# First MoE: activation through Arctan and Sin, in groups of eight steps

## The chip, the cores and the metric

The kernel runs on one core of a Trainium2 chip. Times are microseconds of device time for one execution; "the time" is the median of three runs. TensorE multiplies, VectorE and ScalarE and GpSimd (DVE, ACT and POOL in the rows) work element by element, SyncE's queue (SP) issues all DMAs. PEld is TensorE's load of a stationary operand, which overlaps its multiplying (PE).

## The reference

Three layers over 8 batches of 576 tokens. Packed attention makes 32 packed values per head, and the tokens attend to them. Its result x, 4608 x 512, passes through two feed-forward layers:

```python
h = x @ w_in                                   # 512 -> 2048, weights in float64
sp = np.where(h > 20.0, h, np.log1p(np.exp(np.minimum(h, 20.0))))
g = h * np.tanh(sp)
x2 = g @ w_out                                 # 2048 -> 512
...
logits = x2 @ w_gate                           # second MoE: one of 8 experts per token
expert_idx = np.argmax(logits, axis=1)
for e in range(8):
    ye = np.maximum(xe @ w1[e], 0.0) @ w2[e]   # xe: the tokens of expert e
    out[expert_idx == e] = gate_w * ye
```

## The kernel before, in words

Every float32 product of the two MoEs runs as three matmuls: each operand is split into hi, rounded to 12 bits, and lo, the rest, and hi*hi, hi*lo and lo*hi are summed in PSUM. A split costs one copy (hi) and one two-input subtraction (lo).

Three stages follow each other and overlap at their ends. In the start the keys are attended (Exp on ScalarE), the float64 weights are loaded as 64-bit words and turned into float32 pairs (`convert`), and w_in is multiplied with the packed values (`fold`), so that the first MoE starts from W' = packed values x w_in, one W' per batch, which goes through DRAM (`wp_d`, `wraw`) and is split into `wp` by `get_wp`.

The first MoE works through 16 halves of a batch, 288 tokens each, and 16 steps of 128 middle columns per half: 256 steps. `attend(i)` makes the tokens' split probabilities of a half (scores on TensorE, then VectorE, GpSimd and one Exp on ScalarE). `moe1(n)` makes a pair of steps. `product` multiplies W' with the probabilities into one of two PSUM banks h (six matmuls, L626). The tanh of h/2 goes to `z` (L647) and h itself to `hs` (a copy, L233 or L234), which frees the bank. The activation h * tanh(softplus(h)) is then worked out for both steps of the pair, 128 x 576: with z = sigmoid(-h)^2 = ((1 - tanh(h/2)) / 2)^2 it is h (1 - z) / (1 + z). That takes a Square (L652), an Exp (L654) as a seed of the reciprocal and its scaling (L658), three two-input passes on VectorE (L661, L666, L669), another Square between them (L664), and the split of the result into `g` (a copy, L233, L234 or L236, and a subtraction, L245). `back` multiplies g with w_out into four accumulators (twelve matmuls a step, L637). At the end of a half they are evacuated to `x2f` (L693) and stored.

The second MoE loads one expert per batch, splits its weights (`exh`, `exl`), and does 24 matmuls for each of 128 steps (L885, L905), with a Relu (L892) and one VectorE pass (L897) between them. The gates of the experts need one Exp per half (L763).

The order of the work on every engine is written out ahead by `Plan`. Each `step` names the engines that may do it with an estimated cost, the steps it comes after, the tiles it takes from rings and gives back, and a due time. `Plan.run` plays this through: of the steps that are ready and have their buffers, each engine takes the one that is due first, and where two or three engines could do a step, the one that would end first. The costs set the order alone; on the chip each engine works down its own list and waits for semaphores. `RINGS` holds the number of tiles (h=2, z=3, hs=2, g=2, acc=4). Step n of the first MoE is due at B0 + n * TB (TB = 2897 ns), the outputs LAG = 6 steps later; the second MoE's steps come TC = 3838 ns apart. `copy_ways` lets ScalarE, VectorE or (not from PSUM) GpSimd copy, `tensor_ways` lets GpSimd or VectorE combine two tensors.

ScalarE reads its functions from a loaded table set, and a load is put into the program wherever the next function isn't in the set at hand. The program before has one, ahead of line 218: Exp, Tanh, Square, Relu and Copy all run on it.

## Time and profile before

| | us |
|---|---|
| median of three runs | 1430.24 (1426.92 to 1431.38) |
| span of the profiled execution | 1426.1 |
| TensorE busy (PE) | 1262.9 |
| VectorE busy | 949.8 |
| ScalarE busy | 718.9 |
| GpSimd busy | 575.5 |

The profile is of one execution. A busy share is an average over the three stages, so it has to be read by stretch. A row of the timeline gives the start, the duration, the engine and the line of an instruction, and in brackets how long its engine sat idle ahead of it and what released it. A row of the group table gives the line, engine, operation, tiles out<-in, shapes and count, then the busy time and the mean of one in ns, then the idle time of the engine just before them and what ended it. Matmuls overlap: one of 288 columns has a duration of about 0.3 us but starts 0.13 us after the one ahead.

### The profile page before, as it was taken

What the parts mean: (1) busy time and instruction counts of PE and PEld (TensorE: products, weight loads), DVE (VectorE), ACT (ScalarE), POOL (GpSimd) and SP (SyncE); (2) the same over time, 40 slices, a digit from 0 to 9 for tenths busy, and PEclk for the clock granted to TensorE, in tenths of its full rate; (3) what the DMA queues carried; (4) which work ended last, traced back from release to release, by engine and by line L of the source; (5) the groups of instructions that cost most, each with busy time, mean ns of one, the idle gap of its engine ahead of it and who ended that gap; (6) DMA issues with size and microseconds to landing.
All of it is one profiled execution on the core that took longest, in us unless ns stands there. A gap on an engine that the chain in (4) does not pass through costs nothing.

```text
span 1426.1 us, 23170 instructions
## 1 busy us (share of the span) xinstructions
PE 1262.9 (89%) x8680; PEld 1142.7 (80%) x8681; DVE 949.8 (67%) x1562; ACT 718.9 (50%) x1520; POOL 575.5 (40%) x506
## 2 busy tenths in 40 slices
PE   7776667779889999899998899979999999999997
PEld 4442335568888898888988889879999999999997
DVE  4845455798798786987869878884655456356341
ACT  5553334556676776767777677662323223123120
POOL 2624234574555545555455555572312122022020
PEclk9785558899999999999999999999999999999999
DMA  9854344520021201212012120121525235235130
GB/s 322 293 188 166 132 159 149 192 92 18 32 79 49 78 2 49 78 48 78 2 49 79 49 86 9 56 84 51 169 83 177 95 104 184 74 125 176 43 120 36
DMA packets 59407, 144.51 MB, mean 101 GB/s; under 512 B 6553, under 2 KB 7577, under 8 KB 59289
## 3 DMA queue, kind: packets, MB, share of 16 engines
q1 hardware_dynamic: 59288, 142.97, 29.2%
q8 instruction: 70, 1.15, 0.3%
q14 instruction: 49, 0.39, 0.1%
HBM read 107.23 MB, written 34.66 MB: 99 GB/s over the span
## 4 chain that ended last, share of the span: by engine, by line
PE 35%; DVE 28%; DMA 20%; ACT 7%; issue 5%; POOL 4%; SPq 1%; POOLq 0%; DVEq 0%; ACTq 0%
PE h_p L885 10%; PE y L905 10%; PE x2p L637 8%; DMA eraw<-w 7%; DVE z L661 5%; DVE z L669 5%; DMA word<-w_out 4%; DVE z L666 4%; PE h L626 4%; DMA wp_d<-wst 4%; DMA word<-w_in 2%; ACT z L664 2%; DVE wp L245 2%; DVE g L245 2%; DVE r L658 2%
## 5 line engine op out<-in xcount | busy, mean ns | idle before, releaser
L637 PE MATMUL x2p<-g,woh 128*128 128x288 f32 x2048 | 434.5, 303 | 23.8 <-POOL g L245 17.0
L637 PEld LDWEIGHTS x2p<-g,woh 128*128 128x128 f32 x2048 | 335.9, 192 | 41.9 <-POOL g L245 27.3
L637 PE MATMUL x2p<-g,wol 128*128 128x288 f32 x1024 | 305.7, 299 | 0.9 <-POOL wol L245 0.9
L626 PE MATMUL h<-hl,wp 128*128 128x288 f32 x1536 | 259.5, 308 | 46.3 <-DVE hs L234 19.7
L626 PEld LDWEIGHTS h<-hl,wp 128*128 128x128 f32 x1536 | 226.8, 197 | 58.5 <-ACT hs L233 23.9
L905 PE MATMUL y<-g,exh 128*128 128x288 f32 x1024 | 212.7, 299 | 3.5 <-DVE os L911 3.5
L637 PEld LDWEIGHTS x2p<-g,wol 128*128 128x128 f32 x1024 | 196.7, 192 | 1.2 <-POOL wol L245 1.2
L892 ACT ACTIVATE g<-h_p 128x288 fp32r<-128x288 f32 x128 | 51.9, 406 | 235.4 <-PE h_p L885 209.2
L905 PEld LDWEIGHTS y<-g,exh 128*128 128x128 f32 x1024 | 163.8, 188 | 7.1 <-issue 4.6
L666 DVE SCALAR_TENSOR_TENSOR z<-z,r 128x576 f32<-128x576 f32 x128 | 110.0, 859 | 82.7 <-ACT z L664 82.7
L897 DVE SCALAR_TENSOR_TENSOR g<-h_p,g 128x288 fp32r<-128x288 f32 x128 | 58.1, 454 | 151.2 <-ACT g L892 151.0
L885 PE MATMUL h_p<-x,exh 128*128 128x288 f32 x768 | 156.0, 295 | 0.0
L245 POOL TENSOR_TENSOR g<-z,g 128x576 fp32r<-128x576 f32 x80 | 145.9, 1824 | 17.0 <-ACT g L233 10.7
L905 PE MATMUL y<-g,exl 128*128 128x288 f32 x512 | 151.8, 296 | 0.0
L664 ACT ACTIVATE z<-z,b_m 128x576 f32<-128x576 f32 x128 | 99.4, 777 | 99.6 <-DVE z L661 99.3
L661 DVE SCALAR_TENSOR_TENSOR z<-z,r 128x576 f32<-128x576 f32 x128 | 134.5, 1051 | 14.4 <-POOL r L658 13.3
L647 ACT ACTIVATE z<-h 128x288 f32<-128x288 f32 x256 | 103.1, 404 | 49.2 <-PE h L626 46.8
L885 PEld LDWEIGHTS h_p<-x,exh 128*128 128x128 f32 x768 | 122.9, 188 | 0.0
L669 DVE SCALAR_TENSOR_TENSOR z<-z,hs 128x576 f32<-128x576 f32 x128 | 118.2, 923 | 3.7
L658 POOL TENSOR_SCALAR r<-r 128x576 f32<-128x576 f32 x75 | 59.8, 797 | 137.1 <-ACT r L654 124.9
L654 ACT ACTIVATE r<-z 128x576 f32<-128x576 f32 x128 | 88.0, 688 | 51.0 <-DVE z L666 50.1
L885 PE MATMUL h_p<-x,exl 128*128 128x288 f32 x384 | 112.8, 294 | 0.0
(153 smaller groups left out, 2038.0 us busy)
## 6 DMA issues: line engine op xcount, KB each, us to landing
eraw<-w SPq DMA_DIRECT2D x128, 256.0 KB
wraw<-wp_d SPq DMA_DIRECT2D x60, 256.0 KB
wp_d<-wst SPq DMA_DIRECT2D x48, 256.0 KB
k<-kT SPq DMA_DIRECT2D x16, 640.0 KB
q<-qT SPq DMA_DIRECT2D x32, 288.0 KB
x_d<-x2f SPq DMA_DIRECT2D x16, 576.0 KB
x2f<-x_d SPq DMA_DIRECT2D x16, 576.0 KB
out<-os SPq DMA_DIRECT2D x16, 576.0 KB
```

What stands on the lines that cost most here:

```text
L245: engine.tensor_tensor(out=d, in0=a(), in1=b(), op=op)
L626: T.matmul(out=h, lhsT=wp_t[b, c][:, xw, kt, 128 * (o + k):128 * (o + k) + 128], rhs=a2[i][:, xa, kt], start=(m == 0), stop=(m == 5))
L637: T.matmul(out=accs[i, d], lhsT=w_o[c][xw][:, o + k, 128 * d:128 * d + 128], rhs=t["g"][:, xg, k], start=(f + k == 0 and m == 0), stop=(f ...
L647: z1.append(step("ACT", 291, lambda k=k: S.activation(out=part("z", k), in_=t["p", k], func=AF.Tanh, scale=0.5), after=[ins[n + k], *z1], ...
L654: r0 = step("ACT", 573, lambda: S.activation(out=new("r0"), in_=t["z"], func=AF.Exp, scale=SEED_A), after=[z2], takes=key("r0"), due=due)
L658: engine.tensor_scalar(out=t["r0"], in0=t["r0"], scalar1=SEED_B, scalar2=SEED_C, op0=ALU.mult, op1=ALU.add)
L661: e1 = step("DVE", 669, lambda: V.scalar_tensor_tensor(out=t["z"], in0=t["z"], scalar=1.0, in1=t["r0"], op0=ALU.add, op1=ALU.mult), after= ...
L664: e2 = step("ACT", 573, lambda: S.activation(out=t["z"], in_=t["z"], func=AF.Square, bias=b_m15), after=[e1], due=due)
L666: e3 = step("DVE", 669, lambda: V.scalar_tensor_tensor(out=t["z"], in0=t["z"], scalar=0.75, in1=t["r0"], op0=ALU.add, op1=ALU.mult), after ...
L669: g0 = step("DVE", 669, lambda: V.scalar_tensor_tensor(out=t["z"], in0=t["z"], scalar=-0.5, in1=t["hs"], op0=ALU.add, op1=ALU.mult), after ...
L885: T.matmul(out=h_p, lhsT=ex_t[ek, c][xw][:, k, 128 * o:128 * o + 128], rhs=x2s[xk][:, xx, k], start=(n == 0), stop=(n == 11))
L905: T.matmul(out=accs[xk, d], lhsT=ex_t[ek, 2 + c][xw][:, o, 128 * d:128 * d + 128], rhs=hc[xk, f][:, xh], start=(f == 0 and n == 0), stop=( ...
```

## The change

The activation becomes h * sin(pi/2 - 2 arctan((1 - tanh(h/2)) / 2)), since sin(pi/2 - 2 arctan y) = (1 - y^2) / (1 + y^2). For a pair it is, after the same tanh and copy, an Arctan and a Sin on ScalarE, in place in `z`, and one multiplication on VectorE with `hs`. The two Squares, the Exp, its scaling and two of the three VectorE passes go; `r0` and its ring go with them. The factor 2 of the evacuations is no longer needed.

`moe1` now makes a group of eight steps. First come all eight products with their tanh and copies; the tanh also come after every Sin of the group before (`sins`). Then a Sin of one column (`tables`) stands for the load of the table set, after all the group's tanh; then each pair's Arctan and Sin. The Exp of `attend` and of the first two gates are put between groups by `sins` and `trig_after`. The rings become z=5, hs=4, g=4, the lag of the outputs is a group, and `attend(i + 1)` is planned after the first group of half i.

In the first MoE `tensor_ways(..., False)` leaves two-input passes to VectorE alone: the three of `attend`, the subtraction of `g`, and that of `wp` for all batches but the first. The planner's cost of a matmul goes from 122 to 133 ns (798 for a product, 399 and 1596 for others), TB to 2394, TC to 3192; products within a group are due TI = 798 ns apart. The scratch of dynamic DMAs shrinks. The diff, cut to its core:

```diff
-SEED_A, SEED_B, SEED_C = -1.39926343, 0.65662738, 0.33973963
+GROUP = 8
+HALF_PI = 1.5707963267948966
...
-             q=2, s2=1, mx2=1, sm2=1, at2=1, hl=2, z=3, hs=2, r0=1, g=2, g2=4, x2f=1,
+             q=2, s2=1, mx2=1, sm2=1, at2=1, hl=2, z=5, hs=4, g=4, g2=4, x2f=1,
...
-    def tensor_ways(dst, a, b, op, n):
+    def tensor_ways(dst, a, b, op, n, pool=True):
...
-        return [("Pool", 148 + 2.104 * n, on(G)), ("DVE", 69 + 1.042 * n, on(V))]
+        return [("Pool", 148 + 2.104 * n, on(G))] * pool + [("DVE", 69 + 1.042 * n, on(V))]
...
-    LAG = 6
+    LAG = GROUP
...
-                                               lambda kt=kt: r32(wp_t[b, c][:, 0, kt]), ALU.subtract, 512),
+                                               lambda kt=kt: r32(wp_t[b, c][:, 0, kt]), ALU.subtract, 512, b == 0),
...
+        ex = step("ACT", 573, lambda: S.activation(out=t["s2"], in_=t["s2"], func=AF.Exp, scale=scale),
+                  after=[m3] + sins.get(2 * i - 2, []), due=due)
+        trig_after[2 * i - 1].append(ex)
...
-        z2 = step("ACT", 573, lambda: S.activation(out=t["z"], in_=t["z"], func=AF.Square, bias=b_half, scale=-0.5),
-                  after=z1, due=due)
-        r0 = step("ACT", 573, lambda: S.activation(out=new("r0"), in_=t["z"], func=AF.Exp, scale=SEED_A),
-                  after=[z2], takes=key("r0"), due=due)
-
-        def seed(engine):
-            engine.tensor_scalar(out=t["r0"], in0=t["r0"], scalar1=SEED_B, scalar2=SEED_C, op0=ALU.mult, op1=ALU.add)
-
-        r1 = plan.step([("Pool", 641, lambda: seed(G)), ("DVE", 369, lambda: seed(V))], after=[r0], due=due)
-        e1 = step("DVE", 669, lambda: V.scalar_tensor_tensor(out=t["z"], in0=t["z"], scalar=1.0, in1=t["r0"],
-                                                             op0=ALU.add, op1=ALU.mult),
-                  after=[r1, z2], due=due)
-        e2 = step("ACT", 573, lambda: S.activation(out=t["z"], in_=t["z"], func=AF.Square, bias=b_m15),
-                  after=[e1], due=due)
-        e3 = step("DVE", 669, lambda: V.scalar_tensor_tensor(out=t["z"], in0=t["z"], scalar=0.75, in1=t["r0"],
-                                                             op0=ALU.add, op1=ALU.mult),
-                  after=[e2], frees=key("r0"), due=due)
-        g0 = step("DVE", 669, lambda: V.scalar_tensor_tensor(out=t["z"], in0=t["z"], scalar=-0.5, in1=t["hs"],
-                                                             op0=ALU.add, op1=ALU.mult),
-                  after=[e3, *hc], frees=key("hs"), due=due)
-        g1 = plan.step(copy_ways(lambda: new("g", (128, 2, 2, TK), F32R)[:, 0], lambda: t["z"], 2 * TK), after=[g0],
-                       takes=key("g"), due=due)
-        last_g1 = g1
-        g2 = plan.step(tensor_ways(lambda: t["g"][:, 1], lambda: t["z"], lambda: r32(t["g"][:, 0]), ALU.subtract, 2 * TK),
-                       after=[g1], frees=key("z"), due=due)
...
+        for n in pairs:
+            c = n % 16 // 4
+            z1[n], hc[n] = [], []
+            for k in range(2):
+                at_k = due + (n + k - n0) * TI
+                ins[n + k] = step("PE", 798, lambda n=n, k=k: product(n, k),
+                                  after=wp_done[b, c] + a2_done[i] + [after_in(n + k - 1)],
+                                  takes=[("h", n + k)], frees=[("wa", ("w", b, c))] * (hf == 1 and (n + k) % 4 == 3)
+                                  + [("hl", i)] * ((n + k) % 16 == 15), due=at_k)
+                z1[n].append(step("ACT", 291, lambda n=n, k=k: tanh(n, k), after=[ins[n + k], *z1[n]] + sins.get(gr - 1, []),
+                                  takes=[("z", n)] * (k == 0), due=at_k))
+                hc[n].append(plan.step(copy_ways(lambda n=n, k=k: part(n, "hs", k), lambda n=n, k=k: tiles[n]["p", k], TK, True),
+                                       after=[z1[n][k], *hc[n]], takes=[("hs", n)] * (k == 0), frees=[("h", n + k)], due=at_k))
+                b_steps.extend([z1[n][k], hc[n][k]])
+        due += GROUP * TI
+        tables = step("ACT", 1500, lambda: S.activation(out=trig, in_=b_half, func=AF.Sin),
+                      after=[z for n in pairs for z in z1[n]] + trig_after[gr] + sins.get(gr - 1, []), due=due)
+        sins[gr] = []
+        for j, n in enumerate(pairs):
+            at_n = due + 2 * j * TI
+            z = lambda n=n: tiles[n]["z"]
+            th = step("ACT", 573, lambda z=z: S.activation(out=z(), in_=z(), func=AF.Arctan, bias=b_half, scale=-0.5),
+                      after=[tables, *z1[n]], due=at_n)
+            si = step("ACT", 573, lambda z=z: S.activation(out=z(), in_=z(), func=AF.Sin, bias=b_pi, scale=-2.0),
+                      after=[th], due=at_n)
+            sins[gr].append(si)
+            g0 = step("DVE", 669, lambda n=n, z=z: V.tensor_tensor(out=z(), in0=z(), in1=tiles[n]["hs"], op=ALU.mult),
+                      after=[si, *hc[n]], frees=[("hs", n)], due=at_n)
+            g1 = plan.step(copy_ways(lambda n=n: new(n, "g", (128, 2, 2, TK), F32R)[:, 0], z, 2 * TK), after=[g0],
+                           takes=[("g", n)], due=at_n)
+            last_g1 = g1
+            g2 = plan.step(tensor_ways(lambda n=n: tiles[n]["g"][:, 1], z, lambda n=n: r32(tiles[n]["g"][:, 0]),
+                                       ALU.subtract, 2 * TK, False),
+                           after=[g1], frees=[("z", n)], due=at_n)
+            b_steps.extend([tables, th, si, g0, g1, g2])
+            for k in range(2):
+                c, o = divmod((n + k) % 16, 4)
+                for d in range(4):
+                    outs[n + k, d] = step("PE", 399, lambda n=n, k=k, d=d: back(n, k, d),
+                                          after=[g2, outs.get((n + k - 1, d))] + split["o", c, o],
+                                          takes=[("acc", (i, d))] * (f0 == 0 and n + k == n0),
+                                          frees=[("g", n)] + [("wb", ("o", c, x)) for x in "hl"] * (i == NH - 1 and o == 3),
+                                          due=due + GROUP * TB + (2 * j + k) * (TB - TI))
+                    b_steps.append(outs[n + k, d])
+        due += GROUP * TB
...
-                S.activation(out=x2f[i][:, d], in_=accs[i, d], func=AF.Copy, scale=2.0)
+                S.activation(out=x2f[i][:, d], in_=accs[i, d], func=AF.Copy)
             else:
-                V.tensor_scalar(out=x2f[i][:, d], in0=accs[i, d], scalar1=2.0, scalar2=None, op0=ALU.mult)
+                V.tensor_copy(out=x2f[i][:, d], in_=accs[i, d])
...
-        ex = step("ACT", 113, lambda: gate_exp(i), after=[mx], due=due)
+        ex = step("ACT", 113, lambda: gate_exp(i), after=[mx, *exp_after], due=due)
+        if exp_before is not None:
+            exp_before.append(ex)
...
-    TB, TC = 2897, 3838
+    TB, TI, TC = 2394, 798, 3192
...
+    attend(0, open_b, at(-14))
-        attend(i, after_in(n0 - 17) or open_b, at(n0 - 14))
-        for c in range(4):
-            if hf == 0 and (b, c) not in wp_done:
-                get_wp(b, c, after_in(n0 + 4 * c - 28) or open_b, at(n0 + 4 * c - 12))
-            for f in range(4 * c, 4 * c + 4, 2):
-                moe1(n0 + f, at(n0 + f))
-        if i == 1:
+        for g in range(2):
+            for c in range(2 * g, 2 * g + 2):
+                if hf == 0 and (b, c) not in wp_done:
+                    get_wp(b, c, after_in(n0 + 4 * c - 28) or open_b, at(n0 + 4 * c - 12))
+            moe1(n0 + GROUP * g, at(n0 + GROUP * g))
+            if g == 0 and i + 1 < NH:
+                attend(i + 1, after_in(n0 - 1) or open_b, at(n0 + 2))
+        if i == 2:
             for m in range(2):
-                sp = split_x2(m, m, "x2b", x2_done[m], at(16 * m + 20))
-                b_steps.extend(sp + gate(m, [("x2b", m)], at(16 * m + 24)))
-
-    # the first half again, for the second MoE
+                sp = split_x2(m, m, "x2b", x2_done[m], at(16 * m + 26))
+                b_steps.extend(sp + gate(m, [("x2b", m)], at(16 * m + 28), sins[5], trig_after[6]))
...
-    nc = bacc.Bacc("TRN2", target_bir_lowering=False, num_devices=1)
+    nc = bacc.Bacc("TRN2", target_bir_lowering=False, num_devices=1, dynamic_dma_scratch_size=1024)
```

## Rows read from the trace of the kernel before

**Rows 1.** The page: the busy line, and the chain by engine.
```profile
PE 1262.9 (89%) x8680; PEld 1142.7 (80%) x8681; DVE 949.8 (67%) x1562; ACT 718.9 (50%) x1520; POOL 575.5 (40%) x506
PE 35%; DVE 28%; DMA 20%; ACT 7%; issue 5%; POOL 4%; SPq 1%; POOLq 0%; DVEq 0%; ACTq 0%
```

**Rows 2.** By tile x2p: count, duration min/median/max in ns, first and last start.
```profile
L693 ACT ACTIVATE x2f<-x2p x64: 391/424/456, 297.8 to 981.3; 128x288 f32<-128x288 f32 x64
```

**Rows 3.** By stretch: length, busy us (count) of PE, PEld, DVE, ACT, POOL, PEclk, DMA, GB/s.
```profile
298.00:981.00 683.00, 620.56 (x4439) 592.47 (x4438) 556.08 (x706) 471.17 (x952) 371.46 (x295) 0.98 0.15 52
400.00:935.00 535.00, 491.83 (x3558) 471.03 (x3556) 434.71 (x541) 379.50 (x768) 289.31 (x230) 0.99 0.16 54
```

**Rows 4.** Timeline of TensorE: two products in a row, and the scores of a half.
```profile
942.00 0.95 PE L626 MATMUL h<-hl,wp 128*128 128x288 f32 x6
944.37 0.95 PE L626 MATMUL h<-hl,wp 128*128 128x288 f32 x6
...
614.25 1.19 PE L554 MATMUL o<-q,pkb 128*64 128x288 f32 x8
615.37 0.53 PE L637 MATMUL x2p<-g,woh 128*128 128x288 f32 x2
```

**Rows 5.** Groups by line from 400 to 950 us.
```profile
L637 PEld LDWEIGHTS x2p<-g,woh 128*128 128x128 f32 x1586 | 256.6, 189 | 27.9 <-POOL g L245 23.1 <-issue 2.6 <-ACT x2f L693 1.4
L626 PEld LDWEIGHTS h<-hl,wp 128*128 128x128 f32 x1188 | 168.2, 189 | 33.2 <-DVE hs L234 18.1 <-ACT hs L233 14.9
L245 POOL TENSOR_TENSOR g<-z,g 128x576 fp32r<-128x576 f32 x65 | 119.9, 1845 | 13.6 <-ACT g L233 10.1
L661 DVE SCALAR_TENSOR_TENSOR z<-z,r 128x576 f32<-128x576 f32 x99 | 104.6, 1057 | 12.3 <-POOL r L658 11.4
L669 DVE SCALAR_TENSOR_TENSOR z<-z,hs 128x576 f32<-128x576 f32 x99 | 92.7, 936 | 3.2
L666 DVE SCALAR_TENSOR_TENSOR z<-z,r 128x576 f32<-128x576 f32 x99 | 83.4, 843 | 72.0 <-ACT z L664 72.0
```

**Rows 6.** Timeline of VectorE: two-input passes, GpSimd quiet and at work.
```profile
617.50 0.76 DVE L245 TENSOR_TENSOR g<-z,g 128x576 fp32r<-128x576 f32 x1 [0.17 <-POOL g L236]
618.17 0.75 DVE L661 SCALAR_TENSOR_TENSOR z<-z,r 128x576 f32<-128x576 f32 x1
...
629.18 1.73 DVE L245 TENSOR_TENSOR g<-z,g 128x576 fp32r<-128x576 f32 x1
```

**Rows 7.** Timeline of ScalarE: the one table load, and passes back to back.
```profile
0.78 1.28 ACT L218 ACT_TABLE_LOAD   x1 [0.64 <-PEq L1136]
...
603.56 0.39 ACT L647 ACTIVATE z<-h 128x288 f32<-128x288 f32 x1
603.85 0.40 ACT L233 ACTIVATE hs<-h 128x288 f32<-128x288 f32 x1
...
610.45 0.76 ACT L652 ACTIVATE z<-z,b_half 128x576 f32<-128x576 f32 x1
611.12 0.39 ACT L647 ACTIVATE z<-h 128x288 f32<-128x288 f32 x1
```

**Rows 8.** Timeline: a product with its tanh and copy, and a product that waited.
```profile
640.55 0.96 PE L626 MATMUL h<-hl,wp 128*128 128x288 f32 x6
641.54 0.41 ACT L647 ACTIVATE z<-h 128x288 f32<-128x288 f32 x1 [0.42 <-PE h L626]
641.85 0.41 ACT L233 ACTIVATE hs<-h 128x288 f32<-128x288 f32 x1
...
950.36 1.07 PE L626 MATMUL h<-hl,wp 128*128 128x288 f32 x6 [0.86 <-DVE hs L234]
```

**Rows 9.** By stretch: the end of the first MoE, and the second.
```profile
950.00:968.00 18.00, 12.57 (x70) 11.88 (x71) 17.91 (x19) 8.82 (x19) 13.46 (x11) 0.81 0.20 62
1000.00:1426.00 426.00, 413.25 (x3083) 403.00 (x3081) 210.30 (x508) 106.54 (x233) 81.09 (x70) 0.99 0.34 115
```

**Rows 10.** By stretch, and a piece of the chain: the start.
```profile
283.00:298.00 15.00, 11.96 (x80) 10.28 (x80) 15.00 (x19) 8.79 (x18) 10.20 (x10) 1.00 0.21 74
...
266.54 12.51 DMA word<-w_out
```

More of the change, by code (lines that the diff above doesn't have):

```diff
@@ L633, in back, with part @@
-        def back(k, d):
-            if f + k == 0:
+        def part(n, name, k):
+            return (tiles[n][name] if k else new(n, name))[:, k]
+        def back(n, k, d):
+            f = n % 16 + k
+            c, o = divmod(f, 4)
+            if f == 0:
                 accs[i, d] = tile_of("acc", [128, TK], name=f"x2p{d}")
             for m, (xw, xg) in enumerate(((0, 0), (0, 1), (1, 0))):
-                T.matmul(out=accs[i, d], lhsT=w_o[c][xw][:, o + k, 128 * d:128 * d + 128], rhs=t["g"][:, xg, k],
-                         start=(f + k == 0 and m == 0), stop=(f + k == 15 and m == 2))
@@ L641, in moe1 @@
-        z1, hc = [], []
-        for k in range(2):
-            ins[n + k] = step("PE", 735, lambda k=k: product(k),
-                              after=wp_done[b, c] + a2_done[i] + [after_in(n + k - 1)],
-                              takes=[("h", n + k)], frees=[("wa", ("w", b, c))] * (hf == 1 and o + k == 3)
-                              + [("hl", i)] * (f + k == 15), due=due + k * TB)
-            z1.append(step("ACT", 291, lambda k=k: S.activation(out=part("z", k), in_=t["p", k], func=AF.Tanh, scale=0.5),
-                           after=[ins[n + k], *z1], takes=key("z") * (k == 0), due=due + k * TB))
-            hc.append(plan.step(copy_ways(lambda k=k: part("hs", k), lambda k=k: t["p", k], TK, True), after=[z1[k], *hc],
-                                takes=key("hs") * (k == 0), frees=[("h", n + k)], due=due + k * TB))
@@ L685, in moe1, with tanh @@
-        b_steps.extend([*hc, *z1, z2, r0, r1, e1, e2, e3, g0, g1, g2, *(outs[n + k, d] for k in range(2) for d in range(4))])
-        if f < 14:
+                T.matmul(out=accs[i, d], lhsT=w_o[c][xw][:, o, 128 * d:128 * d + 128], rhs=tiles[n]["g"][:, xg, k],
+                         start=(f == 0 and m == 0), stop=(f == 15 and m == 2))
+        def tanh(n, k):
+            S.activation(out=part(n, "z", k), in_=tiles[n]["p", k], func=AF.Tanh, scale=0.5)
+        for n in pairs:
[12 more added lines that the diff above has]
+                b_steps.extend([z1[n][k], hc[n][k]])
```

61 lines of the change are left out of this document (27 added, 34 removed).

## Prediction

> **What bounds the kernel now.** I read the page's busy line and its chain first [rows 1]. TensorE has 89% of the span, but that is an average over a start that waits for DMAs, a first MoE and a second MoE. The chain gives TensorE 35%, VectorE 28% and DMA 20%, so over long stretches it is VectorE's work that TensorE waits for. The question is how far the first MoE is from TensorE's own pace.
>
> The evacuations of its accumulators (L693) date its halves: the first half ends at 297.8 us, the last of the 16 at 981.3 [rows 2]. That is 683 us for 15 halves, 45.5 us each. The stretch table has the same stretch [rows 3]: 4439 matmuls, VectorE busy 556 of 683 us. Its row from 400 to 935 us has 3558 matmuls in 535 us; a half has 288 of the MoE and 8 for the scores, so these are 12.0 halves of 44.6 us.
>
> What would a half cost on TensorE alone? In an undisturbed stretch one product of six matmuls starts at 942.00 and the next one, behind twelve output matmuls, at 944.37 [rows 4]: 2.37 us for 18 matmuls, 0.132 us each. The scores of a half take from 614.25 to 615.37, 1.12 us. A half is 16 x 2.37 + 1.12 = 39.0 us, and a steady half loses 5.6 us. The group table of 400 to 950 us says where [rows 5]: TensorE's weight loads sit idle 27.9 us ahead of output matmuls, 23.1 of it until GpSimd's subtraction of g (L245, 1.85 us each), and 33.2 us ahead of products, nearly all until a copy of h has freed a bank. Together 61 us in 550, 11%. Both come from the activation: three two-input passes of 0.84 to 1.06 us on VectorE, with waits for other engines between them, then GpSimd's subtraction.
>
> **The change, part by part.**
>
> *VectorE.* L661 and L666 go, one multiplication stays in place of L669, and the second subtraction of g always comes to VectorE. Such a pass takes 0.67 us from its start to its successor's where GpSimd is quiet (617.50 to 618.17) and 1.73 at the worst, with GpSimd at work (629.18) [rows 6]; the mean of the slowest line is 1.06 [rows 5]. I take 0.67, because nearly all two-input work of GpSimd goes, and keep 1.06 as the other end. For 12 halves: VectorE's 434.7 us [rows 3], less 104.6 and 83.4, plus the 65 subtractions moved from GpSimd [rows 5] at 0.67 to 1.06 (44 to 69). The attention's three two-input passes and the weights' four a half are 84 in 12 halves; between none and all of them are new on VectorE (0 to 89). That is 291 to 405 us, 24 to 34 a half. Even the upper end is below 39.0: VectorE leaves the bound. GpSimd keeps only copies of g and casts.
>
> *ScalarE.* Three passes of a pair go, two come. Back to back a 576-column pass with a bias tile takes 0.67 us (610.45 to 611.12), a 288-column one from PSUM 0.29 (603.56 to 603.85) [rows 7]. Removed are two Squares at 0.67 and an Exp without bias tile, between 0.29 and 0.67: 1.63 to 2.01 us. Arctan and Sin add 1.34. ScalarE gets lighter by 0.3 to 0.7 us a pair, 2.3 to 5.4 a half. Against it stand table loads: the trace's only one takes 1.28 us [rows 7], and each group of eight steps needs two, four a half, 5.1 us. With 379.5/12 = 31.6 us a half now [rows 3] that makes 31 to 34, some 80 to 88% of TensorE's 39.0.
>
> [...]
>
> *The cycle of a group.* Grouping adds two waits: no Arctan before the last tanh of its group, no tanh before the last Sin of the group ahead. Queued behind the waiting pass on ScalarE are copies of h, and a copy that waits keeps a PSUM bank and so the next product. Phase A is eight products through two banks. A bank's round is 0.99 us from product start to tanh (640.55 to 641.54), 0.31 on to the copy, 0.41 of copy [rows 8], and at once the next product (950.36 in [rows 8] was released by such a copy): 1.7 us, some 2.0 if the copy is VectorE's and starts after the tanh's 0.41. Two banks make 0.86 to 1.0 us a product, 7 to 8 us a group. Phase B is two loads, eight passes and, as an allowance, 2 us of other copies: 2.6 + 5.4 + 2 = 10 us. The cycle is 17 to 18 us, and TensorE needs 39.0/2 = 19.5. During B it has the previous group's outputs, 8 x 1.58 = 12.7 us, which don't wait for this group's Sins. So the two waits are covered, with about 2 us to spare; each us past that would cost 1 us in each of 30 groups.
>
> *TensorE's order.* Products come in runs of eight, at 0.79 us each quicker than the banks empty (0.86 to 1.0). Outputs of the group ahead can fill the gap; unfilled it costs 0.2 x 8 = 1.7 us a group, filled nothing. The nearest row for a dense stretch is the second MoE: 413.25 busy us in 426 [rows 9], 13 lost over 16 halves. I take 1 us a half, and 0 to 2 for the range.
>
> *The start.* Up to 283 us the float64 weights set the pace (a word DMA of 12.51 us still starts at 266.54), and the change doesn't touch them. From 283 to 298 VectorE is busy all 15 us [rows 10]; less work there could give up to 8 us, and the later first outputs (a group of eight in place of a lag of six steps) could take as much. I take zero.
>
> *The end.* [...] The last group's first output is ready some 6 us after its last tanh (a load, two pairs of passes, three VectorE passes), under 12.7 us of the group ahead. [...] The second MoE runs at TensorE's pace already. The planner's new constants reorder its queues only: plus or minus 5. The smaller edits (factor 2 folded into the Sin form, a constant tile, the scratch size) are priced at nothing; VectorE's and ScalarE's spare 5 us a half cover them, and uncovered they are one small pass in the whole run.
>
> **Sum.** TensorE's own work from 298 to 981 is 4439 x 0.132 = 586 us [rows 3, 4], so 683 - 586 = 97 us can be had. Less 15 halves x 1 us: 82. The profiled span is 1426.1 us and the median of the runs 1430.24, so 4.1 us lie around the span: 1426.1 - 82 + 4.1 = **1348 us**. About 0.3%, 4 us, is what a measurement here can tell from no change.
>
> **Rivals.**
>
> *ScalarE's cycle becomes the bound.* If a switch costs more than its row, or copies of h queue behind Sins, phase B grows. At 21 us a group, 3.5 more than my cycle, a half is 42, the stretch 15 x 42 = 630 and the gain 53: 1377 us. For it: ScalarE's 80 to 88% in two phases that can't overlap. Against it: 2 us to spare and outputs to run meanwhile. [...] 20%.
>
> *Slower: tables switch inside the group.* If Arctan and Sin share no table set, or the copies between them aren't in it, nearly each of the eight passes brings a load. Nine loads in place of two make 17.5 + 7 x 1.28 = 26.5 us a group, 53 a half, 15 x 7.5 = 112 us more: 1542 us. It decides from four extra loads on, 17.5 + 4 x 1.28 = 22.6 us, the present half of 45.5. Against it: in the kernel before Exp, Tanh, Square and Copy live on one load, so functions do share sets; for the new pair no row says it. 5%.
>
> *VectorE stays the bound.* If the moved passes all run at the worst row, 1.73 us, they add 149 x 1.73 = 258 us to 434.7 - 188, 42 us a half, and with the waits between passes the halves stay near 45: 1430 us. Against it: GpSimd, which slows them, has lost its own. 3%, and 2% for gains between this and the first rival.
>
> *Full density* is the forecast's lower tail: 1426 - 97 - 8 + 4 = 1325 us.
>
> **How the numbers follow.** The forecast has 70%, with 1333 to 1364 as its own range (0 to 2 us a half, start and end as above in part). Leaving out the slow cases and the ends of the others, 1333 to 1388 holds 8 in 10: the forecast's range and the greater part of the first rival's. Faster by over 0.3%: 0.70 + 0.20 + 0.02 = 0.92; within 0.3%: 0.03; slower: 0.05.
>
> **What would show it.** Evacuations of the halves 39 to 41 us apart; 365 or more matmuls in each 50 us between 400 and 850; VectorE busy 24 to 34 us a half; 64 table loads of 1.28 us beside the first one; output matmuls that no longer wait for GpSimd. I am wrong if TensorE idles ahead of products until a tanh or a copy of h that waited for a Sin, if the loads number hundreds, or if VectorE's passes stay near 1 us.

## The result, and the profile after

The changed kernel takes 1368.84 us (median; 1366.46 to 1369.12) beside 1428.58 for the kernel before on the same chip (four runs; the 1430.24 further up is the median of three of them), a ratio of 0.9579 (95% interval 0.9555 to 0.9602). The forecast was 1348, its range 1333 to 1388: the sign and the range hold, and the time is 21 us above the forecast. Where these 21 us are is the main question of what follows.

The page first, its busy line and its chain by engine, as in [rows 1]:

```profile
PE 1252.8 (92%) x8680; PEld 1139.5 (83%) x8681; DVE 711.2 (52%) x1328; ACT 705.9 (52%) x1469; POOL 343.3 (25%) x375
PE 64%; DMA 18%; ACT 7%; DVE 6%; issue 2%; SPq 2%; POOL 1%; ACTq 0%; DVEq 0%; POOLq 0%
```

VectorE falls from 67 to 52% of the span and from 28 to 6% of the chain, and TensorE now makes 64% of the chain. The evacuations (L705 now) and two stretches answer to [rows 2] and [rows 3]; columns as there:

```profile
L705 ACT ACTIVATE x2f<-x2p x64: 410/412/414, 310.4 to 908.6; 128x288 f32<-128x288 f32 x64
...
400.00:935.00 535.00, 531.92 (x3953) 516.75 (x3952) 277.46 (x396) 385.11 (x762) 124.26 (x144) 1.00 0.18 60
...
310.40:908.60 598.20, 594.27 (x4412) 575.71 (x4411) 330.12 (x485) 445.51 (x885) 146.00 (x169) 1.00 0.18 59
```

The two evacuations date three parts. The first half ends at 310.4 us in place of 297.8 (12.6 us later). The 15 halves behind it take 598.2 us in place of 683.5 (85.3 less, 39.9 us a half). From the last evacuation to the end it is 1367.4 - 908.6 = 458.8 us in place of 444.8 (14.0 more). Of the 85.3 and of the 14.0, 3.2 us are two products of the second MoE that stood at 968 and 973 us, inside the first MoE, and now come behind it. The sum, 12.6 - 85.3 + 14.0 = -58.7, is the difference of the spans, 1426.1 to 1367.4.

The group table from 400 to 850 us answers to [rows 5]:

```profile
L646 PEld LDWEIGHTS x2p<-g,woh 128*128 128x128 f32 x1434 | 229.1, 188 | 0.0
L633 PEld LDWEIGHTS h<-hl,wp 128*128 128x128 f32 x1080 | 147.2, 188 | 13.3 <-ACT z L650 9.6 <-ACT hs L235 3.7
...
L247 DVE TENSOR_TENSOR g<-z,g 128x576 fp32r<-128x576 f32 x88 | 76.3, 881 | 30.8 <-POOL g L238 30.8
...
L678 DVE TENSOR_TENSOR z<-z,hs 128x576 f32<-128x576 f32 x89 | 64.4, 753 | 97.5 <-ACT z L675 97.5
...
L667 ACT ACT_TABLE_LOAD x23 | 29.5, 1283 | 0.4
```

Output matmuls no longer wait for anybody (27.9 us before); products wait 13.3 us in 450 for the tanh (L650) and the copy of h, 33.2 in 550 before. ScalarE's timeline over one group shows the loads:

```profile
604.39 0.41 ACT L235 ACTIVATE hs<-h 128x288 f32<-128x288 f32 x1
604.82 1.28 ACT L667 ACT_TABLE_LOAD   x1
606.11 0.20 ACT L667 ACTIVATE trig<-b_half 128x1 f32<-128x1 f32 x1
606.22 1.43 ACT L673 ACTIVATE z<-z,b_half 128x576 f32<-128x576 f32 x2
...
610.23 1.43 ACT L675 ACTIVATE z<-z,b_pi 128x576 f32<-128x576 f32 x2
611.67 1.28 ACT L650 ACT_TABLE_LOAD   x1
616.41 0.41 ACT L650 ACTIVATE z<-h 128x288 f32<-128x288 f32 x1 [3.46 <-PE h L633]
```

The load starts 0.02 us after the copy ends at 604.80, and the next pass starts at the load's end. The load back at 611.67 runs while the tanh behind it still waits for its product, so that one is hidden. There are 65 loads in all, each of 1283 ns.

### The profile page after: what moved, and what is told of

Read it like the earlier page. It is cut to its first block, busy times and chain, and to the rows that moved or that the text cites. A ratio compares the mean times of both kernels' runs of the same rounds, so it can differ in the third digit from the quotient of the medians.

```text
span 1367.4 us, 22646 instructions
## 1 busy us (share of the span) xinstructions
PE 1252.8 (92%) x8680; PEld 1139.5 (83%) x8681; DVE 711.2 (52%) x1328; ACT 705.9 (52%) x1469; POOL 343.3 (25%) x375
## 4 chain that ended last, share of the span: by engine, by line
PE 64%; DMA 18%; ACT 7%; DVE 6%; issue 2%; SPq 2%; POOL 1%; ACTq 0%; DVEq 0%; POOLq 0%
PE x2p L646 23%; PE h L633 13%; PE y L919 12%; PE h_p L899 12%; DMA wp_d<-wst 6%; DMA eraw<-w 3%; DMA word<-w_in 3%; DMA word<-w_out 2%; DMA x2f<-x_d 1%; PE o L558 1%; ACT z L673 1%; ACT z L675 1%; SPq L256 1%; DMA wraw<-wp_d 1%; PE l_p L748 1%
## 5 line engine op out<-in xcount | busy, mean ns | idle before, releaser
L646 PE MATMUL x2p<-g,woh 128*128 128x288 f32 x2048 | 420.1, 300 | 3.0 <-POOL g L238 2.0
L633 PE MATMUL h<-hl,wp 128*128 128x288 f32 x1536 | 235.5, 304 | 11.7 <-ACT hs L235 7.5
L633 PEld LDWEIGHTS h<-hl,wp 128*128 128x128 f32 x1536 | 216.2, 194 | 27.5 <-ACT z L650 11.4
L238 POOL TENSOR_SCALAR g<-z 128x576 fp32r<-128x576 f32 x118 | 100.7, 861 | 345.0 <-DVE z L678 229.4
L650 ACT ACTIVATE z<-h 128x288 f32<-128x288 f32 x256 | 105.0, 410 | 121.8 <-PE h L633 114.0
L678 DVE TENSOR_TENSOR z<-z,hs 128x576 f32<-128x576 f32 x128 | 96.3, 781 | 123.9 <-ACT z L675 123.7
L247 DVE TENSOR_TENSOR g<-z,g 128x576 fp32r<-128x576 f32 x128 | 113.6, 901 | 41.1 <-POOL g L238 41.0
L247 DVE TENSOR_TENSOR exl<-eraw,exh 128x512 fp32r<-128x512 f32 x89 | 82.2, 953 | 42.2 <-ACT exh L235 37.3
L235 ACT ACTIVATE hs<-h 128x288 f32<-128x288 f32 x248 | 100.8, 406 | 0.4 <-DVE z L678 0.4
L919 PEld LDWEIGHTS y<-g,exl 128*128 128x128 f32 x512 | 97.2, 190 | 0.0
L235 ACT ACTIVATE exh<-eraw 128x512 fp32r<-128x512 f32 x93 | 58.3, 631 | 70.6 <-DMA eraw<-w 67.4
```

Of the source, the lines that this page charges most:

```text
L235: ways = [("ACT", (51 if psum else 93) + 0.833 * n, on(lambda d, x: S.activation(out=d, in_=x, func=AF.Copy))), ("DVE", 69 + (1.03 if psum ...
L238: ways.append(("Pool", 160 + 0.835 * n, on(lambda d, x: G.tensor_scalar(out=d, in0=x, scalar1=1.0, scalar2=1.0, op0=ALU.mult, op1=ALU.mult))))
L247: engine.tensor_tensor(out=d, in0=a(), in1=b(), op=op)
L633: T.matmul(out=h, lhsT=wp_t[b, c][:, xw, kt, 128 * o:128 * o + 128], rhs=a2[i][:, xa, kt], start=(m == 0), stop=(m == 5))
L646: T.matmul(out=accs[i, d], lhsT=w_o[c][xw][:, o, 128 * d:128 * d + 128], rhs=tiles[n]["g"][:, xg, k], start=(f == 0 and m == 0), stop=(f = ...
L650: S.activation(out=part(n, "z", k), in_=tiles[n]["p", k], func=AF.Tanh, scale=0.5)
```

## The experiments

All kernels side by side. The first evacuation and the last are those of their profiles; the column behind them is the 15 halves between, then the rest of the span behind the last. The times are medians of four runs, of two for two_more_loads and groups_of_four. The ratio is to the kernel before on the same chip.

| kernel | us | ratio (95%) | first | 15 halves | rest |
|---|---|---|---|---|---|
| before | 1428.58 | | 297.8 | 683.5 | 444.8 |
| changed | 1368.84 | 0.9579 (0.9555 to 0.9602) | 310.4 | 598.2 | 458.8 |
| tc_back | 1366.25 | 0.9563 (0.9506 to 0.9619) | 310.1 | 598.2 | 456.3 |
| tc_costs_back | 1359.96 | 0.9546 (0.9482 to 0.9610) | 307.7 | 598.2 | 447.3 |
| costs_back | 1357.19 | 0.9506 (0.9472 to 0.9540) | 307.7 | 598.3 | 446.8 |
| first_half_by_four | 1377.62 | 0.9650 (0.9592 to 0.9708) | 306.4 | 607.6 | 459.7 |
| both_back | 1362.00 | 0.9536 (0.9480 to 0.9591) | 306.2 | 607.2 | 446.8 |
| first_half_as_before | 1348.15 | 0.9442 (0.9414 to 0.9471) | 298.0 | 601.2 | 443.9 |
| gpsimd_again | 1374.89 | 0.9630 (0.9588 to 0.9673) | 309.8 | 604.0 | 459.9 |
| before_vectore_alone | 1392.08 | 0.9754 (0.9712 to 0.9797) | 299.3 | 645.6 | 442.4 |
| before_two_passes_out | 1353.01 | 0.9474 (0.9433 to 0.9514) | 300.9 | 605.6 | 449.6 |
| vectore_alone_gpsimd_loaded | 1460.08 | 1.0226 (1.0175 to 1.0277) | 307.2 | 706.2 | 447.1 |
| two_more_loads | 1407.91 | 0.9860 (0.9804 to 0.9917) | 311.5 | 638.7 | 457.5 |
| groups_of_four | 1393.93 | 0.9757 (0.9718 to 0.9795) | 310.1 | 623.1 | 460.6 |

### The second MoE: the planner's constants

**tc_back** takes back only the distance of the second MoE's steps.

```diff
-    TB, TI, TC = 2394, 798, 3192
+    TB, TI, TC = 2394, 798, 3838
```

> The changed kernel with one constant of the planner set back: TC = 3838 ns, the due spacing of the second MoE's steps. The estimated costs of its matmuls stay new. Theory P: the second MoE lost 14 us (from the last evacuation to the end 458.8 us against 444.8 before) because the planner's new constants order loads and splits of the next batch later; TC alone is enough, then this stretch comes back to 445 to 450 us and the time to about 1357. Rival Q: it is not TC but the matmul costs; then the stretch stays at 456 to 461 and the time at 1369. Rival R: the loss comes from what the first MoE leaves behind (queues, buffers); then it stays as well.

The rest is 456.3 us: the distance alone brings 2.5 us and is not it.

**tc_costs_back** takes back the costs of its matmuls too, and **costs_back** these alone.

```diff
-        y_in[n] = step("PE", 1596, lambda: moe2_in(b, i, f), after=ex_done[b, c] + x2_split_done[i] + [None if early else ins[N1 - 1]],
+        y_in[n] = step("PE", 1473, lambda: moe2_in(b, i, f), after=ex_done[b, c] + x2_split_done[i] + [None if early else ins[N1 - 1]],
...
-            y_out[n, d] = step("PE", 399, lambda d=d: moe2_out(b, i, f, d),
+            y_out[n, d] = step("PE", 366, lambda d=d: moe2_out(b, i, f, d),
```

> The changed kernel with TC = 3838 ns and the second MoE's estimated matmul costs set back too (1473 and 366 ns); the first MoE is planned as in the changed kernel. Theory P and Q: the second MoE's stretch comes back to 444 to 448 us, time about 1356. Rival R (the first MoE's leavings): it stays at 456 to 461 and the time at 1369.

> The changed kernel with the planner's costs of the second MoE's matmuls alone taken back (1473 and 366 for 1596 and 399); its steps stay due 3192 ns apart. Theory C (the costs alone make the worse order in the second MoE): from the last evacuation to the end 444 to 450 us in place of 458.8, the time 1357 to 1364. Rival B (it takes both, costs and distance, to come back to the old order): 453 to 460 us, the time 1364 to 1371.

The rest falls to 447.3 and 446.8 us, so the costs alone do it, some 12 of the 14.0 us, and what the first MoE leaves behind (rival R) is not it. They emit the same matmuls in another order. The stretch from 1000 to 1300 us, the y matmuls and the VectorE share of the split of x2, first for the changed kernel, then for costs_back:

```profile
1000.00:1300.00 300.00, 290.83 (x2121) 282.69 (x2121) 151.62 (x356) 76.16 (x166) 69.35 (x55) 0.98 0.36 119
...
L919 PE MATMUL y<-g,exh 128*128 128x288 f32 x666 | 141.0, 303 | 8.1 <-DVE os L925 8.0
...
L730 DVE TENSOR_TENSOR x<-x2f,x 128x576 fp32r<-128x576 f32 x7 | 13.0, 1860 | 0.2
```

```profile
1000.00:1300.00 300.00, 295.90 (x2205) 288.35 (x2205) 156.16 (x372) 82.66 (x178) 64.19 (x57) 1.00 0.40 129
...
L919 PE MATMUL y<-g,exh 128*128 128x288 f32 x696 | 145.1, 300 | 1.8 <-DVE os L925 1.8
...
L730 DVE TENSOR_TENSOR x<-x2f,x 128x576 fp32r<-128x576 f32 x2 | 3.7, 1866 | 0.1
```

With the change's costs 84 matmuls fewer are done in 300 us. TensorE waits 8.0 us for VectorE's evacuation of y (L925), seven of the 1.86 us subtractions of L730 into x stand on VectorE where costs_back has two, and the granted clock is 0.98. Which entry of the lists starts the loss, this subtraction or the loads of the expert's weights ahead of it, no run separates. The new cost of 133 ns a matmul is what [rows 4] show, 0.132 us, and the old 122 is not: the truer cost gave the worse order.

### The start: groups against late weights

The first half's products wait for the quarters of W', which arrive one by one. The changed kernel's stretch that answers to [rows 10], then ScalarE and TensorE near 280 us:

```profile
283.00:298.00 15.00, 8.84 (x39) 7.15 (x40) 12.93 (x17) 9.16 (x17) 7.86 (x8) 0.66 0.42 138
...
250.61 0.41 ACT L650 ACTIVATE z<-h 128x288 f32<-128x288 f32 x1
...
273.77 0.63 ACT L235 ACTIVATE wp<-wraw 128x512 fp32r<-128x512 f32 x1 [5.13 <-DMA wraw<-wp_d]
274.31 0.39 ACT L650 ACTIVATE z<-h 128x288 f32<-128x288 f32 x1
...
280.11 1.28 ACT L667 ACT_TABLE_LOAD   x1
...
286.14 2.19 PE L558 MATMUL o<-q,pkb 128*64 128x288 f32 x8 [4.89 <-DMA q<-qT]
290.29 0.61 PE L646 MATMUL x2p<-g,woh 128*128 128x288 f32 x1 [1.96 <-POOL g L238]
```

The tanh at 250.61 is that of step 11, so steps 8 to 11 were ready for their Arctan at 251 us. But it comes after the tanh of steps 12 to 15. The first of these stands on ScalarE behind a cast of W' that waits 5.13 us for its DMA, and starts at 274.31; the load for the whole group is at 280.11, 29 us late for half of it. Until 290.29 TensorE has no output to make: 39 matmuls in these 15 us where before had 80, and the granted clock is 0.66 in this stretch, 1.00 before [rows 10].

**first_half_by_four** makes four groups of four of the first half, and plans the attention of the second half behind step 12 in place of step 8.

```diff
+        size = 4 if i == 0 else 8
+        for f in range(0, 16, size):
...
-            moe1(n0 + GROUP * g, at(n0 + GROUP * g))
+            moe1(n0 + f, at(n0 + f), size)
```

> The changed kernel with the first half of the first batch in four groups of four steps, all other halves in groups of eight. Theory G: the first half ends 12.6 us later than before (310.4 against 297.8 us) because the Arctans of steps 8 to 11, whose products are through at 251 us, wait for the products of steps 12 to 15, whose weights land at 273; by four, steps 8 to 11 go ahead: the half ends at 298 to 304 and the time is 1358 to 1364. Rival S: the start is set by the float64 weights' DMAs and the other order of the queues, not by the group; then the half ends at 309 to 312 and the time is 1369 or, for four more table loads of 1.28 us, up to 1374.

The first half does end 4.0 us earlier, short of the 298 to 304 expected, and the kernel is slower. From the timelines of TensorE and ScalarE:

```profile
276.32 0.43 PE L649 MATMUL x2p<-g,woh 128*128 128x288 f32 x2
...
282.34 0.68 ACT L409 ACTIVATE a<-word 128x512 f32<-128x512 f32 x1 [3.32 <-DMA word<-w_out]
282.93 0.39 ACT L653 ACTIVATE z<-h 128x288 f32<-128x288 f32 x1
...
292.69 3.25 PE L636 MATMUL h<-hl,wp 128*128 128x288 f32 x12 [5.01 <-ACT hs L235]
295.74 0.68 PE L649 MATMUL x2p<-g,woh 128*128 128x288 f32 x2
...
317.43 4.69 PE L636 MATMUL h<-hl,wp 128*128 128x288 f32 x18 [2.46 <-ACT hs L235]
```

The outputs of steps 8 to 11 do come earlier, from 276.32 in place of 290.29. But the last two tanh of the group of steps 12 to 15 stand on ScalarE behind a conversion of w_out that waits 3.32 us for its DMA (282.34). Behind them come the load, the Arctans and Sins and the split of g, two products of the second half go ahead on TensorE (292.69), and the outputs of that group start at 295.74 only. So the theory's wait is there, but taking it away brings little by itself. The second half's products wait for copies of h behind the added loads and Sins, and the second half takes 50.5 us from one first evacuation to the next (306.44 to 356.98) where the changed kernel takes 41.3 (310.41 to 351.69): nearly all of the 9.4 us by which the 15 halves are longer (607.6). **both_back** joins this with tc_costs_back:

> The first half by four and the second MoE's TC and costs set back, together. If theories G and P (or Q) both hold, the gains add up, since they lie in different stretches: 1369 - 8 - 13 = 1348 us, which is the time that was forecast for the change with neither loss. If only one holds, about 1357; if neither, 1369.

It has both effects side by side, 607.2 and 446.8 us, and misses the 1348 expected. With these constants the groups of four bring the first half's end forward by 1.5 us only (307.7 to 306.2).

**first_half_as_before** removes the group from the first half altogether: pairs, the seed by Exp, the Squares and the three VectorE passes, outputs six steps behind; groups from the second half on, and the planner's costs and distance as in tc_costs_back. The first half's own matmuls are planned at the old costs too.

```diff
-            moe1(n0 + GROUP * g, at(n0 + GROUP * g))
+                if i == 0:
+                    for f in range(4 * c, 4 * c + 4, 2):
+                        moe1_pair(f, at(f))
+            if i > 0:
+                moe1(n0 + GROUP * g, at(n0 + GROUP * g))
```

> The changed kernel with the planner's constants of the second MoE taken back (as in tc_costs_back), and with the first half alone worked as before: pairs of steps, outputs six steps behind, seed by Exp, Squares and three VectorE passes (the seed in a tile of hs), its evacuations doubled; GpSimd takes no two-input pass there either. Groups of eight from the second half on. Theory G (the start loses because a group holds the outputs of steps 8 to 15 back until W' of its last quarter is there): the first half ends at 298 to 302 in place of 307.7, the other 15 halves and the second MoE stay (598 and 447 us): span 1343 to 1347, time 1346 to 1354. Rival P (the loss of the start is the planner's order or VectorE alone, not the group): the first half still ends at 306 to 309, time 1356 to 1364. Rival L (the loss only moves: the first group of the second half then waits instead): first half at 298 to 302, but the last evacuation still at 904 to 909, time 1355 to 1364.

```profile
L793 ACT ACTIVATE x2f<-x2p x60: 410/411/415, 342.2 to 899.2; 128x288 f32<-128x288 f32 x60
L795 DVE TENSOR_SCALAR x2f<-x2p x4: 448/458/458, 298.0 to 300.5; 128x288 f32<-128x288 f32 x4
...
283.00:298.00 15.00, 15.00 (x95) 13.79 (x95) 13.24 (x18) 9.52 (x21) 8.26 (x8) 0.85 0.24 85
```

The first half ends at 298.0, TensorE is busy through the stretch (95 matmuls), and the last evacuation comes 6.7 us ahead of that of tc_costs_back: 1348.15 us. So of the 12.6 us that the start lost the group costs 9.7 (307.7 to 298.0, with the same constants of the second MoE), and the order made by those constants the rest (310.4 to 307.7). Of the 9.7 us 3.0 are lost again in the 15 halves behind (601.2 for 598.2), and the rest of the span is 3.4 us shorter (443.9 for 447.3), for which no run gives a reason. What in the group costs the 9.7 is shown in part only: ending the wait of steps 8 to 11 for the tanh of steps 12 to 15 gives 1.5 to 4.0 back in the groups of four, less what their added loads cost, and how much falls to the loads, to the Sins and to the order of the queues stays open. This kernel is faster than both the kernel before and the changed one.

### The first MoE: which part brings the 85 us

**before_two_passes_out** leaves out L661 and L666 of the kernel before, **before_vectore_alone** moves the two-input passes there to VectorE, and **gpsimd_again** lets GpSimd have them in the changed kernel.

```diff
-        e1 = step("DVE", 669, lambda: V.scalar_tensor_tensor(out=t["z"], in0=t["z"], scalar=1.0, in1=t["r0"],
...
-        e3 = step("DVE", 669, lambda: V.scalar_tensor_tensor(out=t["z"], in0=t["z"], scalar=0.75, in1=t["r0"],
...
```

> The kernel before without the two VectorE passes at L661 and L666: the pair goes from the scaled seed to the second Square and on to the last multiplication, so the activation's values are not the reference's. No groups, no table loads, GpSimd as before, planner's constants as before. Theory A (VectorE's passes and the waits between them are most of the 5.6 us that a half loses; the start and the second MoE lose nothing without groups and new constants): VectorE falls by 188 us in 12 halves, halves of 41 to 42.5 us, first half's end within 3 us of 297.8, second MoE within 4 us of 444.8: time 1365 to 1385. Rival B (GpSimd's subtraction is the stall): its 23 us in 12 halves stay, halves of 43 to 44.5: 1395 to 1415.

The group table from 400 to 850 us:

```profile
L637 PEld LDWEIGHTS x2p<-g,woh 128*128 128x128 f32 x1434 | 229.0, 188 | 8.1 <-issue 7.4 <-ACT x2f L687 0.5
...
L626 PEld LDWEIGHTS h<-hl,wp 128*128 128x128 f32 x1074 | 152.0, 188 | 5.0 <-DVE hs L234 5.0
...
L245 DVE TENSOR_TENSOR g<-z,g 128x576 fp32r<-128x576 f32 x79 | 61.7, 782 | 122.7 <-POOL g L236 122.7
...
L245 POOL TENSOR_TENSOR g<-z,g 128x576 fp32r<-128x576 f32 x11 | 15.7, 1430 | 0.9
```

Two passes less, with no table load and no group, make halves of 40.4 us, a little under theory A's 41 to 42.5, and the start and the rest stay near those of before. But the run does not set the passes apart from GpSimd: with VectorE freed, the planner gives it 79 subtractions of g in these 450 us and GpSimd 11, where GpSimd had 65 in 550 [rows 5]. Rival B's stall went with the passes.

```diff
-        return [("Pool", 148 + 2.104 * n, on(G)), ("DVE", 69 + 1.042 * n, on(V))]
+        return [("Pool", 148 + 2.104 * n, on(G))] * pool + [("DVE", 69 + 1.042 * n, on(V))]
...
-        g2 = plan.step(tensor_ways(lambda: t["g"][:, 1], lambda: t["z"], lambda: r32(t["g"][:, 0]), ALU.subtract, 2 * TK),
+        g2 = plan.step(tensor_ways(lambda: t["g"][:, 1], lambda: t["z"], lambda: r32(t["g"][:, 0]), ALU.subtract, 2 * TK, False),
```

> The kernel before with one part of the change alone: the two-input passes of the attention, of g and of W' (all batches but the first) on VectorE alone. Theory A (VectorE is the bound before, its load must fall first): VectorE gets 44 to 69 us of subtractions in 12 halves and up to 89 us of the attention's and weights' passes on top of 434.7, some 40 to 49 us a half against the present 44.6; no gain, and slower if its load passes the half: 1425 to 1490. Rival B (the wait for GpSimd's subtraction is the stall, and passes without GpSimd run at 0.67 us): the 23 us of waits in 12 halves go, 1395 to 1410.

The same stretch, 400 to 850 us:

```profile
L637 PEld LDWEIGHTS x2p<-g,woh 128*128 128x128 f32 x1382 | 222.3, 188 | 14.3 <-DVE g L245 8.4 <-issue 4.4 <-DVE z L661 0.4
...
L661 DVE SCALAR_TENSOR_TENSOR z<-z,r 128x576 f32<-128x576 f32 x87 | 73.8, 848 | 3.5 <-POOL r L658 3.1
L245 DVE TENSOR_TENSOR g<-z,g 128x576 fp32r<-128x576 f32 x87 | 71.6, 823 | 1.9 <-POOL g L236 1.3
```

This one surprised: VectorE gets more work and the halves fall to 43.0 us, 37.9 us in the first MoE; theory A fell, and 1392.08 is even a little under rival B's 1395. L661 takes 848 ns in place of 1057 [rows 5], and the wait for GpSimd's subtraction of g is gone.

For gpsimd_again the same is turned round in the changed kernel, here for g:

```diff
-                                       ALU.subtract, 2 * TK, False),
+                                       ALU.subtract, 2 * TK),
```

> The changed kernel, but GpSimd may take two-input passes in the first MoE again; groups of eight and the Arctan and Sin stay. Theory A (the gain comes from the shorter activation; the outputs of the group ahead give each subtraction of g some 12 us of cover, so a slow GpSimd subtraction costs little): the 15 halves from the first evacuation to the last stay at 598 to 613 us, the time is 1366 to 1384. Rival B (the gain comes from GpSimd no longer standing ahead of the output matmuls and slowing VectorE): the waits of the outputs for GpSimd come back, about 23 us in 12 halves, and VectorE's passes go back to about 1 us: 25 to 45 us more, 1392 to 1412.

The same stretch again:

```profile
L646 PEld LDWEIGHTS x2p<-g,woh 128*128 128x128 f32 x1414 | 225.9, 188 | 0.0
...
L247 POOL TENSOR_TENSOR g<-z,g 128x576 fp32r<-128x576 f32 x23 | 35.2, 1530 | 1.4
```

With the short activation the same freedom costs 5.8 us in 15 halves, as theory A had it. GpSimd has 23 subtractions of g in 450 us, and the output matmuls wait for none of them. So the parts overlap: moving the passes alone brings 37.9 us, the short activation in groups with GpSimd left free 79.5 (683.5 to 604.0), both together 85.3, the two products that moved being in the last two figures. But the planner used the freedom less than before: 23 subtractions in 450 us where GpSimd had 65 in 550. No run has the short activation with GpSimd's old load.

**vectore_alone_gpsimd_loaded** asks which of GpSimd's two effects before_vectore_alone removed.

```diff
+        if n // 2 % 3 < 2:
+            step("Pool", 1360, lambda: G.tensor_tensor(out=idle, in0=idle, in1=idle, op=ALU.subtract), after=[g0], due=due)
```

> As before_vectore_alone (1392.1 us; the two-input passes on VectorE alone), but GpSimd gets, in two pairs of steps of three, a subtraction of 128 x 576 of its own on a tile that nobody else reads: as much two-input work as the subtraction of g gave it before, with no TensorE work behind it. GpSimd's copies can queue behind it, and the planner sees its cost. Theory D (VectorE's passes last longer while GpSimd runs a two-input pass, and that is what the kernel before lost by them): VectorE's three passes of a pair go back from 0.77 to 0.85 us to 0.85 to 1.05, and the time to 1412 to 1440. Rival C (the loss was GpSimd's 1.85 us in the chain ahead of the output matmuls, which this kernel doesn't have): passes stay at 0.77 to 0.87 us, time 1388 to 1402.

A subtraction for which nobody waits costs 68 us, more than theory D's range (1412 to 1440), and rival C is out. From the group table from 400 to 850 us, and a piece of the timeline of VectorE and GpSimd:

```profile
L663 DVE SCALAR_TENSOR_TENSOR z<-z,r 128x576 f32<-128x576 f32 x78 | 86.7, 1111 | 5.3 <-POOL r L660 5.1
...
L688 POOL TENSOR_TENSOR idle<-idle 128x576 f32<-128x576 f32 x52 | 68.7, 1320 | 0.4
...
600.88 1.64 POOL L688 TENSOR_TENSOR idle<-idle 128x576 f32<-128x576 f32 x1
601.44 1.70 DVE L247 TENSOR_TENSOR g<-z,g 128x576 fp32r<-128x576 f32 x1
...
605.48 0.75 DVE L247 TENSOR_TENSOR g<-z,g 128x576 fp32r<-128x576 f32 x1
```

L663 (L661 before) goes from 848 to 1111 ns. The four two-input passes of a pair (the three and the subtraction of g) go from 3.24 to 3.59 us by their means; over 120 pairs that makes, as an estimate, 42 of the 60.6 us by which the 15 halves are longer. Not every pass suffers: the second of the three is at 751 ns, 796 without the load. The subtraction of g at 601.44 ends at 603.14, 0.62 us after GpSimd's pass ends at 602.52; at 605.48, with GpSimd quiet, it takes 0.75. So by these rows VectorE's pass lost 0.95 us of the 1.08 that it shared with GpSimd's. Part of the 68 us is another thing: GpSimd takes 6 copies of g in 450 us in place of 36, and VectorE 32 in place of 18. The size measured is that of both together.

### ScalarE's cycle and the size of the group

**two_more_loads** adds an Exp and a Sin of one column behind the Sin that stands for the load.

```diff
-        tables = step("ACT", 1500, lambda: S.activation(out=trig, in_=b_half, func=AF.Sin),
+        tables = step("ACT", 1500, lambda: [S.activation(out=trig, in_=b_half, func=AF.Sin), S.activation(out=trig, in_=b_half, func=AF.Exp), S.activation(out=trig, in_=b_half, func=AF.Sin)],
```

> The changed kernel with one more Exp and Sin of one column behind the Sin that stands for the table load, so two more loads in each group of eight: 2 x 1.28 us and two passes of about 0.2 us, 2.97 us of ScalarE a group, 31 groups, order otherwise the same. Theory A (the group's cycle on ScalarE has about 2 us of cover, as the prediction reckoned from 17.5 and 19.5 us): about 1 us a group is exposed, 30 us: 1390 to 1405. Rival B (ScalarE's cycle is already the bound): all is exposed, 92 us: about 1460. Rival C (ScalarE's idle time of 3.5 us in one group of a half and 2.4 in the other takes nearly all of it): 0 to 10 us, 1367 to 1380.

```profile
610.64 1.28 ACT L667 ACT_TABLE_LOAD   x1
611.94 0.20 ACT L667 ACTIVATE trig<-b_half 128x1 f32<-128x1 f32 x1
612.16 1.28 ACT L667 ACT_TABLE_LOAD   x1
...
L633 PEld LDWEIGHTS h<-hl,wp 128*128 128x128 f32 x1008 | 145.7, 199 | 33.4 <-ACT hs L235 25.1 <-issue 8.3
```

The 15 halves take 40.5 us more, 1.35 us in each of 30 groups for 2.97 us of ScalarE: 1.6 us were covered. The time, 1407.91, is just past theory A's 1405. Products wait for copies of h, as rival 1 of the prediction had it.

From the start of one load to that of the next it is 1.52 us (610.64 to 612.16): 1.28 of load, 0.20 of the pass between them and 0.04 besides. So a switch costs little more than its row here.

**groups_of_four** halves the group.

```diff
+        size = 4
+        for f in range(0, 16, size):
```

> The changed kernel in groups of four steps throughout: twice the table loads, some 128 and one, and twice as often the wait of the tanh for the Sins. Theory A (only the loads cost: two more loads in eight steps took 41 us in two_more_loads): 1395 to 1412. Rival B (the phases are shorter too, so that ScalarE's wait for the first product of a group comes twice as often and the outputs have half the cover): 1415 to 1450. Rival C (the smaller group starts its Sins earlier and pays for its loads with that): 1366 to 1385.

At 1393.93 us it is just under theory A's 1395, and further from the others. Its 15 halves take 623.1 us, 24.9 more than in groups of eight, less than the 40.5 of the same number of loads added to a group of eight. What gives the difference back (fewer Sins at a time between the tanhs, or passes that the short groups overlap) no run separates.

## Why the prediction was right or wrong

**The 15 halves.** Forecast 39.0 us of TensorE's own work and 0 to 2 lost a half, 1 taken; measured 39.9. The gain forecast was 82 us, the gain measured 85.3, of which 3.2 are the two products that moved behind the stretch. This step was right.

**VectorE.** Forecast 24 to 34 us a half, measured 330.12/15 = 22.0, below the range; the multiplication takes 753 ns, its unhindered value in [rows 6], and the subtraction of g 881. The sum left out that the seed's scaling (L658) goes from VectorE too, 19.8 us from 400 to 850 us, and that the planner hands copies round: of the copies of h VectorE made 41 there and now makes 6, and of those of g GpSimd makes 82 in place of 30. It also took passes counted over 550 us from a busy time of 535, about 4 us that change nothing. That VectorE leaves the bound was right. What I did not see is how much longer VectorE's passes took beside GpSimd's two-input work (1057 ns for L661 in [rows 5], 848 without it): I priced the moved passes as a burden of 44 to 158 us in 12 halves, and in the kernel before moving them alone gains 37.9 us in 15.

**ScalarE and the cycle.** Forecast 31 to 34 us a half, measured 445.51/15 = 29.7, a little below, as ScalarE makes no copy of g from 400 to 850 us where it made 40; 64 loads beside the first, at 1.28 us, as forecast. I reckoned 2 us of cover for the two waits of a group, and two_more_loads found 1.6. Rival 1 was a near thing and not what happened: its price of 1377 lies near the measured time by chance, since the waits of products are 13.3 us in 450, 1.2 a half, inside the 0 to 2 of the forecast.

**The start: the step that failed first.** I set a gain of up to 8 us from VectorE's lighter work against a loss of as much from later first outputs and took zero. The loss was 12.6 us, and first_half_as_before, with the old constants of the second MoE, gives it back to within 0.2 (298.0 and 297.8). Two things were missed. The group holds the first half's outputs back, 9.7 us; part of this is that they wait for the tanh of the group's last step, which in the start stands behind weights that come late, and the rest is not taken apart. And VectorE, busy all 15 us in [rows 10], was no bound there: before_two_passes_out, with two passes a pair less on it, ends the first half at 300.9.

**The second MoE: the other one.** "The planner's new constants reorder its queues only: plus or minus 5" was mis-sized: 14.0 us, 3.2 of it moved work, and the costs alone take 12.0 back (458.8 to 446.8). A new order was worth more than the five I gave it.

**The sum.** 12.6 and 10.8 us (14.0 less 3.2) were missed, and the 4.1 us that I put around the span were too many: here the median is 1.4 above the span (1368.84 - 1367.4). In every run of the changed kernel it is 1.7 to 1.8 from the span to the time of the same run, so the 4.1 was probably for the greater part a profiled execution below the median, not time around the span. 1348 + 23.4 - 2.7 = 1368.7. With both missed terms taken back, first_half_as_before has 1348.15 us. That it meets the forecast so closely is luck in part: its 15 halves are 3.0 us longer than the changed kernel's, and its rest 3.4 shorter than that of tc_costs_back.

**The other rivals.** Tables did not switch inside the group: Arctan, Sin and the copies between them run on one load (L667, 32 loads for 32 groups). VectorE did not stay the bound.

## What to carry to other kernels

Where work is batched to save a cost of switching, ask for each batch when its last input arrives: in a steady stretch other work can cover the wait (here for eight steps; groups of four cost 24.9 us more), and where inputs trickle in the batch holds its outputs back, so that the old form may be kept there. Two-input work on GpSimd was no free capacity here beside a VectorE that does two-input passes (its first pass of a pair went from 848 to 1111 ns), and moving it to the busier engine made the kernel shorter (1392 us, a ratio of 0.9754). A constant that only orders the queues is a change in its own right and wants a run of its own.

## What the runs showed of the hardware

With a GpSimd subtraction of 1.32 us, for which nothing waits, in two of three pairs, VectorE's first pass of a pair took 263 ns longer in the mean (848 to 1111); one subtraction beside it took 1.70 us, and 0.75 with GpSimd quiet. A table load took 1283 ns in the kernel before and in every kernel with groups. In the changed kernel it started 0.02 us after the end of the pass ahead (604.80 to 604.82), and the load back to the old set at 611.67 ran while the pass behind it still waited for its input, so that it cost nothing: 3.46 us of waiting were left behind it.
